# Delta-rule attention with two feed-forward blocks: inverse blocks through TensorE, doubling in the solve, an order table per task

## Chip, cores and metric

One core of one Trainium2 chip runs the whole program. The metric is the device time of one execution in microseconds (us). TensorE does matmuls, VectorE (DVE in the profile) and ScalarE (ACT) element-wise work, GpSimd (POOL) also element-wise work, and SyncE (SP) issues DMAs.

## What is computed

```python
# q, k, v: (4, 8, 768, 48); beta: (4, 8, 768)
k_n = k / (norm(k, axis=-1) + 1e-6)
for t in range(768):                              # per batch and head
    y[t] = q[t] @ state                           # state: 48 x 48
    state += beta[t] * outer(k_n[t], v[t] - k_n[t] @ state)
x = y, heads side by side                         # 3072 tokens x 384
h = x @ moe_w_in                                  # 384 x 2048
g = where(h >= 1, h, where(h <= -1, 0, (h + 1)**2 / 4))
x = g @ moe_w_out                                 # 2048 x 384
xn = x / sqrt(mean(x*x) + 1e-6) * rms_g
return (silu(xn @ w_gate) * (xn @ w_val)) @ w_out # 384 x 1536, back to 384
```

q, k, v and beta are float32, the weights 64-bit floats, which are decoded on the chip into a high and a low part, so that each product is three matmuls.

## The kernel before, in words

The sequence is cut into 12 chunks of 64 tokens. A unit u is one chunk c = u // 2 for half of the batch (p = u % 2); its tiles hold two batch elements on the two halves of the 128 partitions and eight heads beside each other. Within a chunk the recurrence is a triangular system: the Gram matrix of the keys, scaled by beta and the norms, is inverted, and everything else is matmuls.

The work is written as generator tasks. Each `yield S(engine, cost, needs, acquire, release)` is a stage, with an estimated cost and the buffers (tokens) that it takes and returns. `Flow` (lines 57 to 160) runs over all tasks when the program is built, simulates the engines with these costs and so fixes the order of instructions on each engine. A task's priority is the one given in `fl.add` plus an offset from the table `PLACE`, which is kept by chunk, feature block or group. Names in `CHAIN` go ahead of everything when they are ready. On TensorE lateness counts first; then `KEEP` and `STAY` favour staying with the kind of matmul that runs, small tiles (`TILED`) or full ones.

The tasks: `a_ss` loads k and sums its squares, `a_coef` (line 381) makes the coefficients, `ka_load` loads transposed keys, and `a_gram` (line 415) computes the Gram blocks (tile gk). For the groups g = 0 and 1 (chunks 0 and 1) `a_gram` scales them into al (L438), stores them to DRAM (L440) and keeps a masked copy off (L444). `inv16` then inverts the 16x16 diagonal blocks of a whole chunk: eight gathers from DRAM put one block on each partition (L469), 15 steps of two operations solve (L475, L481; on VectorE for chunk 0, on GpSimd for chunk 1), a copy (L483) and two DMAs through DRAM (L486, L489) bring the inverse back as c, and L499 multiplies it into dt. Later chunks go through `inverse`, `a_mz` and `a_mw`, with GpSimd as the solver (L526, L532). The attention itself is `b_load`, `b_q`, `b_vn`, `b_gs`, `b_tr`, `b_x`, `b_ds`; `b_xT` transposes the result into xh and xl. `b_tr` of chunks 0 and 1 multiplies with dt (L640) and off (L648).

The first feed-forward block is `m1(j, f)` over seven token blocks j (the first two are one chunk of 256 tokens each, then two chunks each) and 16 feature blocks f: hps, the activation on ScalarE and VectorE (L780 to L791), then acc three features behind; all big matmuls are L743 to L745. A weight piece comes through `w_dec`: a load (L279), three ScalarE operations (L286 to L288) and three more (L296, L302 or L300, L304). The 32 pieces of the first block stay in the 32 buffers of the pool wp, which before that also lends its buffers to early tiles (`early`). SyncE's queue is in order. The stages that load weights, keys or queries name `("inv16", 0, 1)` or `("inv16", 0, 19)` among their needs, that is the gathers or the end of chunk 0's solve. Until the first `m1`, gaps on TensorE are filled with dummy matmuls on the tile warm (L876). From `m2_l1` on the second feed-forward block runs in a fixed order without the planner.

## Time and profile before

| | us |
|---|---|
| median of three runs | 1097.67 (1097.43 to 1098.48) |
| profiled execution | 1095.42 |
| its span, first to last instruction | 1093.7 |
| TensorE matmul busy | 1071.0 (98%) |
| VectorE busy | 625.6 (57%) |
| ScalarE busy | 517.1 (47%) |
| GpSimd busy | 261.2 (24%) |

A stretch is read with the windows view, which gives each engine's busy time in it and the granted TensorE clock as a share of full speed. Dummy matmuls count as busy, and a busy matmul may overlap the next one, so the distance from start to start tells what one costs. The timeline view gives the order of instructions with start, duration and, in brackets, the idle time before and what ended it.

### The profile page before, as it was taken

What the parts mean: (1) busy time and instruction counts of PE and PEld (TensorE: products, weight loads), DVE (VectorE), ACT (ScalarE), POOL (GpSimd) and SP (SyncE); (2) the same over time, 40 slices, a digit from 0 to 9 for tenths busy, and PEclk for the clock granted to TensorE, in tenths of its full rate; (3) what the DMA queues carried; (4) which work ended last, traced back from release to release, by engine and by line L of the source; (5) the groups of instructions that cost most, each with busy time, mean ns of one, the idle gap of its engine ahead of it and who ended that gap; (6) DMA issues with size and microseconds to landing.
All of it is one profiled execution on the core that took longest, in us unless ns stands there. A gap on an engine that the chain in (4) does not pass through costs nothing.

```text
span 1093.7 us, 23824 instructions
## 1 busy us (share of the span) xinstructions
PE 1071.0 (98%) x9872; PEld 905.7 (83%) x9872; DVE 625.6 (57%) x1132; ACT 517.1 (47%) x981; POOL 261.2 (24%) x438
## 2 busy tenths in 40 slices
PE   8989799999999999999999999999999999999998
PEld 8878798988887888888888888888888888888886
DVE  6878988866677656855666533633333333333332
ACT  4676866756556557557656542522222122222221
POOL 3137849478286581100000000000000000000000
PEclk9998999999999999999999999999999999999999
DMA  7896575865755725353334930100010010010000
GB/s 220 268 283 191 130 174 170 192 179 165 191 163 135 206 88 128 115 165 107 109 114 174 330 111 10 40 30 29 0 39 20 1 49 10 22 36 1 30 1 29
DMA packets 156700, 121.84 MB, mean 111 GB/s; under 512 B 111408, under 2 KB 122288, under 8 KB 156592
## 3 DMA queue, kind: packets, MB, share of 16 engines
q1 hardware_dynamic: 134400, 117.60, 36.0%
q10 hardware_dynamic: 22192, 2.72, 1.8%
q8 instruction: 78, 1.28, 0.5%
q14 instruction: 30, 0.25, 0.1%
HBM read 86.21 MB, written 34.08 MB: 110 GB/s over the span
## 4 chain that ended last, share of the span: by engine, by line
PE 87%; DVE 4%; DMA 4%; ACT 2%; issue 1%; SPq 1%; POOL 0%; ACTq 0%; DVEq 0%; POOLq 0%
PE acc L743 11%; PE acc L744 10%; PE acc L745 10%; PE gv L744 9%; PE gv L743 9%; PE gv L745 9%; PE hps L743 6%; PE hps L744 6%; PE hps L745 6%; PE gs L619 3%; PE tr L683 2%; PE px L696 2%; PE ds L710 1%; DMA kvb<-in_kv 1%; PE mg L575 1%
## 5 line engine op out<-in xcount | busy, mean ns | idle before, releaser
L743 PE MATMUL acc<-g,w 128*128 128x512 f32 (+1 forms) x552 | 209.6, 380 | 0.0
L744 PE MATMUL acc<-g,w 128*128 128x512 f32 (+1 forms) x552 | 205.2, 372 | 0.3 <-DVE g L791 0.3
L745 PE MATMUL acc<-g,w 128*128 128x512 f32 (+1 forms) x552 | 204.7, 371 | 0.0
L745 PE MATMUL gv<-fix,w 128*128 128x512 f32 x432 | 168.1, 389 | 0.0
L743 PE MATMUL gv<-fix,w 128*128 128x512 f32 x432 | 168.0, 389 | 0.0
L744 PE MATMUL gv<-fix,w 128*128 128x512 f32 x432 | 168.0, 389 | 0.0
L760 ACT ACTIVATE g<-fix 128x512 fp32r<-128x512 f32 x72 | 45.4, 631 | 211.4 <-PE acc L745 203.9
L743 PE MATMUL hps<-xh,w 128*128 128x512 f32 (+1 forms) x336 | 126.1, 375 | 0.3 <-DVE s L783 0.3
L761 DVE TENSOR_TENSOR g<-fix,g 128x512 fp32r<-128x512 f32 x72 | 49.9, 693 | 131.8 <-ACT g L760 131.8
L744 PE MATMUL hps<-xl,w 128*128 128x512 f32 (+1 forms) x336 | 121.5, 362 | 0.0
L745 PE MATMUL hps<-xh,w 128*128 128x512 f32 (+1 forms) x336 | 121.4, 361 | 0.0
L743 PEld LDWEIGHTS acc<-g,w 128*128 128x128 f32 x552 | 103.8, 188 | 20.4
L745 PEld LDWEIGHTS acc<-g,w 128*128 128x128 f32 x552 | 103.9, 188 | 18.2
L744 PEld LDWEIGHTS acc<-g,w 128*128 128x128 f32 x552 | 103.9, 188 | 17.4 <-DVE g L791 0.7
L783 DVE TENSOR_TENSOR s<-s,hps 128x512 f32<-128x512 f32 (+1 forms) x112 | 67.8, 608 | 86.3 <-ACT s L781 85.4
L780 ACT ACTIVATE s<-hps 128x512 f32<-128x512 f32 (+1 forms) x112 | 59.8, 534 | 108.6 <-PE hps L745 96.2
L526 POOL TENSOR_TENSOR tmp<-nt,xi 128x31 f32<-128x31 f32 (+15 forms) x155 | 92.8, 599 | 46.7 <-DMA nt<-scr_a 35.0
L983 DVE TENSOR_TENSOR fix<-fix,gv 128x512 f32<-128x512 f32 x72 | 49.5, 687 | 87.4 <-ACT fix L982 87.4
L532 POOL TENSOR_TENSOR xi<-xi,tmp 128x31 f32<-128x31 f32 (+15 forms) x155 | 94.2, 608 | 12.1
L743 PEld LDWEIGHTS gv<-fix,w 128*128 128x128 f32 x432 | 81.1, 188 | 16.9
L745 PEld LDWEIGHTS gv<-fix,w 128*128 128x128 f32 x432 | 81.1, 188 | 16.8
L744 PEld LDWEIGHTS gv<-fix,w 128*128 128x128 f32 x432 | 81.1, 188 | 16.7
(162 smaller groups left out, 1648.5 us busy)
## 6 DMA issues: line engine op xcount, KB each, us to landing
wst<-in_w SPq DMA_DIRECT2D x68, 384.0 KB
w2d<-wst SPq DMA_DIRECT2D x36, 384.0 KB
w<-w2d SPq DMA_DIRECT2D x36, 384.0 KB
kvb<-in_kv SPq DMA_DIRECT2D x22, 384.0 KB
kt<-in_kqT SPq DMA_DIRECT2D x24, 256.0 KB
scr_a<-al SPq DMA_DIRECT2D x24, 256.0 KB
qs<-in_kqT SPq DMA_DIRECT2D x48, 128.0 KB
xn_d<-x SPq DMA_DIRECT2D x12, 384.0 KB
```

Source lines behind the costliest of these rows:

```text
L526: nc.gpsimd.tensor_tensor(out=tv, in0=nt[:, m:32, j:m].to_broadcast([w, n, m]), in1=x[:, j:m, 0:m].to_broadcast([w, n, m]), op=ALU.mult,)
L532: nc.gpsimd.tensor_tensor(out=x[:, m:32, 0:m], in0=x[:, m:32, 0:m], in1=tv, op=ALU.add)
L619: nc.tensor.matmul(out=ps[half(b), h, 0:n], lhsT=kt[u][half(1 - b), 4 * k + h, :], rhs=qs[p][half(1 - b), b, 4 * k + h, 0:n], start=True, ...
L683: nc.tensor.matmul(out=ps[half(b), h, 0:D], lhsT=w[half(b), h, :], rhs=r[half(b), h, :], start=True, stop=True)
L743: nc.tensor.matmul(out=out, lhsT=wh, rhs=xh, start=first, stop=False, skip_group_check=shared)
L744: nc.tensor.matmul(out=out, lhsT=wh, rhs=xl, start=False, stop=False, skip_group_check=shared)
L745: nc.tensor.matmul(out=out, lhsT=wl, rhs=xh, start=False, stop=last, skip_group_check=shared)
L760: nc.scalar.activation(out=hi, in_=src, func=ACTF.Copy)
L761: nc.vector.tensor_tensor(out=lo, in0=src, in1=hi.bitcast(F32), op=ALU.subtract)
L780: nc.scalar.activation(out=s, in_=ps, func=IDENTITY_SAT240, scale=240.0)
L783: nc.vector.tensor_tensor(out=s, in0=s, in1=ps, op=ALU.max)
L983: nc.vector.tensor_tensor(out=sg, in0=sg, in1=ps[0], op=ALU.mult)
```

## The change

For chunks 0 and 1 the scaled Gram block no longer goes through DRAM. `a_gram` writes e1, the block times a table mcoef that keeps only the diagonal 16x16 blocks (coefficients and signs included). `inv16` gathers with 64 matmuls of e1 against a selection matrix pick_t into PSUM (tile nps), which a copy brings to nt. The solve writes into x as before; for chunk 0 it now inverts 4x4 blocks in three steps and then doubles the size twice (4 to 8, 8 to 16), each with two products and two sums; chunk 1 keeps the 15 steps on GpSimd. A new task `inv_t` spreads x with a mask mlow (e2) and brings it back with 32 matmuls against pick_g (tile cps), from which dt is made. The constant tables come from the identity matrix with five VectorE operations. The first loads of k are issued at the very start, those of kt on ScalarE's queue. The needs that name `inv16` at other tasks' loads are gone. `PLACE` has an entry for every task, in the order in which tasks are added; `CHAIN` is longer, and `KEEP`, `STAY` and `AHEAD` are other numbers. In the diff the table and repeated edits are left out.

```diff
--- before.py
+++ after.py
-    TILED = ("a_gram", "a_mw", "b_gs", "b_tr", "b_x", "b_ds")
-    CHAIN = {"b_tr": 2, "b_x": 6, "inverse": 3, "inv16": 2, "a_mz": 2, "a_mw": 3, "b_gs": 1, "a_ss": 2, "b_ds": 1, "a_gram": 1}
-    DRAIN, SWITCH, KEEP, STAY, AHEAD = 0.15, 0.22, 25.96, 0, 0.17
+    TILED = ("a_gram", "a_mw", "b_gs", "b_tr", "b_x", "b_ds", "inv16", "inv_t")
+    CHAIN = {"a_gram": 6, "a_mw": 3, "a_mz": 9, "a_ss": 3, "b_ds": 3, "b_gs": 3, "b_load": 28, "b_q": 7, "b_tr": 9, "b_vn": 6, "b_x": 2, "b_xT": 30, "inv16": 13, "inv_t": 18, "inverse": 3, "w_in": 12, "x_load": 14}
+    DRAIN, SWITCH, KEEP, STAY, AHEAD = 0.15, 0.22, 229.72, 19.85, 0.27
     PLACE = {
...
     }
     def add(self, prio, fn, *args):
         gen, n = fn(*args), fn.__name__
+        i = self.seen[n] = self.seen.get(n, -1) + 1
         if n in self.PLACE:
-            prio += self.PLACE[n][args[0] // 2 if n in self.BY_UNIT else args[0]]
+            prio += self.PLACE[n][i]
         self.live.append([prio, (n, *args), gen, next(gen), 0])
 
...
     mdiag = cst([128, 4], "mdiag")
+    mlow = cst([128, 4], "mlow")
+    pick_t = cst([128, 16], "pick_t")
+    pick_g = cst([128, 16], "pick_g")
+    mcoef = [cst([128, 2 * H, 4], f"mcoef{c}") for c in range(2)]
...
     def consts():
+        for p in range(NP):
+            kv_b[p] = p2.tile([128, 2, DM], F32, name="kvb", tag="kvb")
+            nc.sync.dma_start(out=kv_b[p][:, 0], in_=kv[p, 0, :, 0])
         nc.sync.dma_start(out=beta_sb, in_=beta)
+        for p in range(NP):
+            kt[p] = p2.tile([128, H, C], F32, name="kt", tag="kt")
+            nc.scalar.dma_start(out=kt[p], in_=kqT[p, 0, :, 0])
...
     def consts2():
+        make_identity(nc, ident)
+        neg = early([128, C], "neg")
+        nc.vector.scalar_tensor_tensor(out=neg, in0=ident[:, 0:C], scalar=-1.0, in1=ident[:, C:], op0=ALU.mult, op1=ALU.subtract)
+        for t, v in (
+            (mdiag, neg.rearrange("p (x t) -> p x t", t=16)), (pick_t, neg.rearrange("p (x t) -> p t x", t=16)),
+            (pick_g, neg.rearrange("p (g x) -> p g x", x=4)), (mlow, neg.rearrange("p (g x) -> p x g", x=4)),
+        ):
+            nc.vector.reduce_sum(t, v, axis=mybir.AxisListType.X)
...
             needs = [("a_gram", EARLY - 1)] if f + SK * i > 14 else []
-        if n == 1:
-            needs = needs + ([("inv16", 0, 1 if f + SK * i < 9 else 19)] if f + SK * i >= 4 else [])
...
-            yield S("SP", (1, 0.55), [("inv16", 0, 1 if u < 4 else 19)], mem)
+            yield S("SP", (1, 0.55), (), mem)
...
+        if g < 2:
+            nc.vector.tensor_tensor(
+                out=mcoef[g], in0=bc(nn.rearrange("p u h -> p (u h)"), 4), in1=mdiag.unsqueeze(1).to_broadcast([128, 2 * H, 4]), op=ALU.mult
+            )
+            return
...
-            yield S("SP", (1, 0.73), (), ("kt",))
-            ka_t[u] = kt[u] = p2.tile([128, H, C], F32, name="kt", tag="kt")
-            nc.sync.dma_start(out=kt[u], in_=kqT[p, c, :, 0])
+            yield S("SP", (0, 0.73), (), ("kt",))
+            ka_t[u] = kt[u]
...
-        if g > 1:
-            yield S("ACT", 1.7, [("a_coef", g)], ("wp" if ew else "al",), ("at",), alt=[("DVE", 0.68)])
-        else:
-            yield S("DVE", 0.68, [("a_coef", g)], ("wp",))
+        if g < 2:
+            yield S("DVE", 0.7, [("a_coef", g)], ("wp",))
+            off["e", u] = e1 = early([128, 16 * 4 * H], "e1")
+            nc.vector.tensor_tensor(
+                out=e1.rearrange("p (s m) -> p m s", s=16), in0=ps.rearrange("p h (x s) -> p (h x) s", s=16),
+                in1=bc(mcoef[g][:, H * i:H * i + H].rearrange("p h x -> p (h x)"), 16), op=ALU.mult,
+            )
+            yield S("DVE", 0.68, [("inv16", 0, 0)] + ([("a_gram", u - 1)] if u else []), ("wp",) if g else ("wt",), (bank, "wp") if u == 3 else (bank,))
+            off[u] = early([128, H, C], "off") if g else p2.tile([128, H, C], F32, name="off", tag="wt")
+            nc.vector.tensor_tensor(out=off[u], in0=ps, in1=off["m"].unsqueeze(1).to_broadcast([128, H, C]), op=ALU.mult)
+            return
+        yield S("ACT", 1.7, [("a_coef", g)], ("wp" if ew else "al",), ("at",), alt=[("DVE", 0.68)])
...
     def inv16(c):
         us = (2 * c, 2 * c + 1)
-        name, eng = ("POOL", nc.gpsimd) if c else ("DVE", nc.vector)
         if c:
-            yield S("POOL", 1.0, [("inv16", 0)], ("tx", "tx", "z", "z"))
-        else:
-            yield S("POOL", 2.0, (), ("tx", "tx", "z", "z", "wp"))
+            yield S("POOL", 1.0, [("inv16", 0)], ("tx", "tx", "wp"))
+        else:
+            yield S("POOL", 1.4, (), ("tx", "tx", "wp", "wp"))
             off["m"] = moff = early([128, C], "moff")
             nc.gpsimd.memset(moff, -1.0)
-            nc.gpsimd.memset(mdiag, -1.0)
             for b in range(2):
-                for t, base, pat, cm in ((moff, -16, [[-16, 4], [0, 16]], 1), (mdiag, 0, [[-16, 4]], 1), (mdiag, 15, [[16, 4]], -1)):
-                    nc.gpsimd.affine_select(
-                        out=t[half(b)], in_=t[half(b)], compare_op=ALU.is_ge, fill=0.0, base=base, pattern=pat, channel_multiplier=cm
-                    )
-        x = p2.tile([128, 16, 16], F32, name="x0", tag="tx")
+                nc.gpsimd.affine_select(
+                    out=moff[half(b)], in_=moff[half(b)], compare_op=ALU.is_ge, fill=0.0, base=-16, pattern=[[-16, 4], [0, 16]], channel_multiplier=1
+                )
+        nt, x = (p2.tile([128, 272], F32, name=nm, tag=tag) for nm, tag in (("nt0", "g21"), ("x0", "tx")))
+        off["x", c] = x
+        xv, nv = (t[:, 0:256].rearrange("p (t s) -> p t s", s=16) for t in (x, nt))
         nc.gpsimd.memset(x, 0.0)
-        nc.gpsimd.affine_select(out=x, in_=x, compare_op=ALU.not_equal, fill=1.0, base=0, pattern=[[1, 16], [-1, 16]], channel_multiplier=0)
-        yield S("SP", (5, 2.4), [("a_gram", u, 2) for u in us])
-        nt = p2.tile([128, 16, 16], F32, name="nt0", tag="g21")
-        for k in range(8):
-            o, r = 16 * k, 16 * (k % 4)
-            q = nc.scalar if k in (1, 3, 5) else nc.sync
-            q.dma_start(out=nt[o:o + 16], in_=scr_a[c][o:o + 16, :, :, r:r + 16].rearrange("t u h s -> (u h) t s"))
-        tmp = p2.tile([128, 64], F32, name="tmp0", tag="tx")
-        for j in range(15):
-            n, m = 15 - j, j + 1
-            yield S(name, 0.5 + n * m * 0.006 if c else 0.37 + n * m * 2 / 960)
-            tv = tmp[:, 0:n * m].rearrange("p (a b) -> p a b", a=n)
-            eng.tensor_tensor(
+        nc.gpsimd.affine_select(out=xv, in_=xv, compare_op=ALU.not_equal, fill=1.0, base=0, pattern=[[1, 16], [-1, 16]], channel_multiplier=0)
+        for k, u in enumerate(us):
+            yield S("PE", 1.35, [("a_gram", u, 1)], () if k else ("at",), ("wp",))
+            if k == 0:
+                ps = ap_.tile([128, 16, 16], F32, name="nps", tag="at")
+            e1 = off.pop(("e", u)).rearrange("p (s m) -> p s m", s=16)
+            for r in range(16):
+                for b in range(2):
+                    o = 64 * b + 32 * k
+                    nc.tensor.matmul(out=ps[o:o + 32, r, :], lhsT=e1[half(b), r, :], rhs=pick_t[half(b)], start=True, stop=True)
+        yield S("ACT" if c else "DVE", 0.43, (), (), ("at",))
+        if c:
+            nc.scalar.activation(out=nv, in_=ps.rearrange("p s t -> p t s"), func=ACTF.Copy)
+        else:
+            nc.vector.tensor_copy(nv, ps.rearrange("p s t -> p t s"))
+        tmp = early([128, 512], "tmp0")
+        if c:
+            for j in range(15):
+                n, m = 15 - j, j + 1
+                yield S("POOL", 0.45 + n * m * 0.0058)
+                tv = tmp[:, 0:n * m].rearrange("p (a b) -> p a b", a=n)
+                nc.gpsimd.tensor_tensor(
+                    out=tv,
+                    in0=nv[:, m:16, j:m].to_broadcast([128, n, m]),
+                    in1=xv[:, j:m, 0:m].to_broadcast([128, n, m]),
+                    op=ALU.mult,
+                )
+                nc.gpsimd.tensor_tensor(out=xv[:, m:16, 0:m], in0=xv[:, m:16, 0:m], in1=tv, op=ALU.add)
+            return
+
+        def blocks(t, w):
+            return t.rearrange("p (k r) -> p k r", r=17 * w)[:, :, 0:16 * w].rearrange("p k (t s) -> p k t s", s=16)
+
+        n4, x4 = blocks(nt, 4), blocks(x, 4)
+        for j in range(3):
+            n, m = 3 - j, j + 1
+            yield S("DVE", 0.4)
+            tv = tmp[:, 0:4 * n * m].rearrange("p (k a b) -> p k a b", k=4, a=n)
+            nc.vector.tensor_tensor(
                 out=tv,
-                in0=nt[:, m:16, j:m].to_broadcast([128, n, m]),
-                in1=x[:, j:m, 0:m].to_broadcast([128, n, m]),
+                in0=n4[:, :, m:4, j:m].to_broadcast([128, 4, n, m]),
+                in1=x4[:, :, j:m, 0:m].to_broadcast([128, 4, n, m]),
                 op=ALU.mult,
             )
-            eng.tensor_tensor(out=x[:, m:16, 0:m], in0=x[:, m:16, 0:m], in1=tv, op=ALU.add)
-        yield S("DVE", 0.6)
-        nc.vector.tensor_copy(nt, x.rearrange("p t s -> p s t"))
-        yield S("SP", (1, 1.5))
-        scr = dram.tile([16, 8, 2, H, 16], F32, name=f"scr_{c}", tag=f"scr_{c}")
-        nc.sync.dma_start(out=scr.rearrange("s x u h t -> (x u h) s t"), in_=nt)
-        yield S("SP", (1, 0.5))
-        inv["c"] = cc = p2.tile([128, 2 * H, 16], F32, name="c0", tag="z")
-        nc.sync.dma_start(out=cc, in_=scr.rearrange("s x u h t -> x s (u h t)"))
-        yield S("DVE", 1.08, ["consts2"], ("x2",))
-        m = p2.tile([128, 2 * H, 4], F32, name="m0", tag="g21")
-        nn = coef[c][1].rearrange("p u h -> p (u h)")
-        nc.vector.tensor_tensor(out=m, in0=bc(nn, 4), in1=mdiag.unsqueeze(1).to_broadcast([128, 2 * H, 4]), op=ALU.mult)
+            nc.vector.tensor_tensor(out=x4[:, :, m:4, 0:m], in0=x4[:, :, m:4, 0:m], in1=tv, op=ALU.add)
+        half_t = p2.tile([128, 64], F32, name="half", tag="tx")
+        for w in (4, 8):
+            q = 8 // w
+            nw, xw = blocks(nt, 2 * w), blocks(x, 2 * w)
+            tv = tmp[:, 0:q * w**3].rearrange("p (k i j l) -> p k i j l", k=q, i=w, j=w)
+            hv = half_t[:, 0:q * w * w].rearrange("p (k i j) -> p k i j", k=q, i=w)
+            for lhs, rhs, out in ((nw[:, :, w:2 * w, 0:w], xw[:, :, 0:w, 0:w], hv), (xw[:, :, w:2 * w, w:2 * w], hv, xw[:, :, w:2 * w, 0:w])):
+                yield S("DVE", 0.37 + 2 * q * w**3 / 960)
+                for k in range(q):
+                    nc.vector.tensor_tensor(
+                        out=tv[:, k],
+                        in0=lhs[:, k].unsqueeze(2).to_broadcast([128, w, w, w]),
+                        in1=rhs[:, k].rearrange("p l j -> p j l").unsqueeze(1).to_broadcast([128, w, w, w]),
+                        op=ALU.mult,
+                    )
+                nc.vector.reduce_sum(out, tv, axis=mybir.AxisListType.X)
+
+    def inv_t(c, i):
+        yield S("POOL" if c else "DVE", 1.1 if c else 0.72, [("inv16", c)], ("wp",))
+        eng = nc.gpsimd if c else nc.vector
+        e2 = early([128, 512], "e2").rearrange("p (t x s) -> p t x s", t=8, x=4)
+        xv = off["x", c][:, 128 * i:128 * i + 128].rearrange("p (t s) -> p t s", s=16)
+        eng.tensor_tensor(
+            out=e2, in0=xv.unsqueeze(2).to_broadcast([128, 8, 4, 16]),
+            in1=bc(mlow, 16).unsqueeze(1).to_broadcast([128, 8, 4, 16]), op=ALU.mult,
+        )
+        yield S("PE", 1.15, [("inv_t", c, 0)] if i else (), () if i else ("at",), ("wp",) if i else ("wp",))
+        if i == 0:
+            off["c", c] = ap_.tile([128, 16, 16], F32, name="cps", tag="at")
+        ps = off["c", c]
+        for t in range(8):
+            for b in range(2):
+                nc.tensor.matmul(
+                    out=ps[half(b), 8 * i + t, :], lhsT=e2[half(b), t].rearrange("p x s -> p (x s)"), rhs=pick_g[half(b)], start=True, stop=True
+                )
+        if i == 0:
+            return
         inv[c] = x2p.tile([128, 2 * H, 4, 16], F32, name="dt", tag="x2")
+        cc = ps.rearrange("p t g -> p g t")
         for p in range(2):
             hs = slice(H * p, H * p + H)
-            if p:
-                yield S("DVE", 0.69, (), (), ("tx", "tx", "z", "z"))
+            yield S("DVE", 0.69, (), () if p else ("x2",), ("at", "tx", "tx", "wp") if p else ())
             nc.vector.tensor_tensor(
                 out=inv[c][:, hs],
                 in0=cc[:, hs].unsqueeze(2).to_broadcast([128, H, 4, 16]),
-                in1=m[:, hs].unsqueeze(3).to_broadcast([128, H, 4, 16]),
+                in1=mcoef[c][:, hs].unsqueeze(3).to_broadcast([128, H, 4, 16]),
                 op=ALU.mult,
             )
 
...
-            yield S("PE", 0.98, [("inv16", c, 20 + p), ("b_vn", u)] + gs, ("at",))
+            yield S("PE", 0.98, [("inv_t", c, 1, 2 + p), ("b_vn", u)] + gs, ("at",))
...
+            for i in range(2 * (g < 2)):
+                fl.add(p0 + 7 + i, inv_t, g, i)
```

## Rows read from the trace of the kernel before

**Rows 1.** Windows, busy us: PE, PEld, DVE, ACT, POOL (x instructions); clock, DMA share, GB/s

```profile
0.00:5.00 5.00, 2.77 (x13) 2.78 (x14) 0.54 (x9) 2.58 (x5) 3.81 (x21) 1.00 0.46 141
5.00:20.00 15.00, 14.86 (x167) 14.49 (x167) 10.26 (x22) 8.22 (x18) 4.37 (x5) 1.00 0.70 222
20.00:66.00 46.00, 42.47 (x921) 39.34 (x920) 39.95 (x103) 26.48 (x59) 12.73 (x34) 1.00 0.93 277
66.00:140.00 74.00, 63.27 (x955) 58.14 (x955) 63.37 (x126) 55.01 (x123) 44.34 (x67) 0.93 0.67 181
140.00:200.00 60.00, 58.52 (x1074) 55.43 (x1070) 52.05 (x113) 38.84 (x95) 43.05 (x72) 1.00 0.69 188
200.00:600.00 400.00, 399.29 (x4595) 330.25 (x4594) 266.04 (x478) 248.74 (x460) 152.86 (x240) 1.00 0.52 147
```

**Rows 2.** Windows of the filler matmuls alone (tile warm), TensorE, to 66 us

```profile
0.00:66.00 66.00, 32.75 (x248) 30.54 (x248) 1.00 0.84 254
```

**Rows 3.** Timeline, chunk 0: start us, us, engine, line, operation, operands, count [idle before]

```profile
8.69 0.69 DVE L438 TENSOR_TENSOR al<-gk,nn 128x512 f32<-128x512 f32 x1 [0.90 <-PE gk L427]
...
20.12 0.17 DVE L475 TENSOR_TENSOR tmp<-nt,x 128x15 f32<-128x15 f32 x1
...
27.94 0.48 DVE L483 COPY nt<-x 128x256 f32<-128x256 f32 x1
...
28.45 0.39 SPq L486 DMA_DIRECT2D scr<-nt  x1
...
31.96 0.69 SPq L489 DMA_DIRECT2D c<-scr  x1
...
36.47 1.29 DVE L499 TENSOR_TENSOR dt<-c,m 128x512 f32<-128x512 f32 x2
...
37.78 2.07 PE L640 MATMUL tr<-kvb,dt 64*64 64x48 f32 x64
...
64.80 0.39 PE L743 MATMUL hps<-xh,w 128*128 128x256 f32 x1
```

**Rows 4.** Timeline and chain of work, chunk 1: GpSimd, a load, two TensorE waits

```profile
50.23 0.24 POOL L475 TENSOR_TENSOR tmp<-nt,x 128x15 f32<-128x15 f32 x1 [21.38 <-DVE w L302]
...
73.46 7.09 DMA c<-scr
...
83.35 1.95 PE L640 MATMUL tr<-kvb,dt 64*64 64x48 f32 x32 [3.52 <-DVE qs L629]
...
134.62 1.76 PE L619 MATMUL gs<-qs,kt 64*64 64x112 f32 x16 [2.44 <-DVE qs L629]
```

**Rows 5.** Groups by line, L304 (busy us, mean ns), 9-66 and 87-137 us; timeline, last one

```profile
L304 DVE TENSOR_TENSOR w<-dy,w 128x384 fp32r<-128x384 f32 x13 | 7.6, 606 | 0.2
...
L304 DVE TENSOR_TENSOR w<-dy,w 128x384 fp32r<-128x384 f32 x14 | 11.0, 783 | 0.3
...
139.22 0.56 DVE L304 TENSOR_TENSOR w<-dy,w 128x384 fp32r<-128x384 f32 x1
```

**Rows 6.** Groups by form, VectorE solve step, 20 to 28.5 us: busy, mean ns

```profile
L475 DVE TENSOR_TENSOR tmp<-nt,x 128x64 f32<-128x64 f32 x1 | 0.8, 818 | 0.0
...
L475 DVE TENSOR_TENSOR tmp<-nt,x 128x63 f32<-128x63 f32 x2 | 0.4, 224 | 0.1
```

**Rows 7.** Timeline, TensorE, one change to small matmuls and back

```profile
149.99 0.28 PE L744 MATMUL hps<-xl,w 128*128 128x256 f32 x1
150.11 0.28 PE L745 MATMUL hps<-xh,w 128*128 128x256 f32 x1
150.32 1.20 PE L565 MATMUL mg<-tx,g 32*32 32x32 f32 x64
151.45 0.38 PE L743 MATMUL acc<-g,w 128*128 128x256 f32 x1
151.67 0.28 PE L744 MATMUL acc<-g,w 128*128 128x256 f32 x1
151.79 0.28 PE L745 MATMUL acc<-g,w 128*128 128x256 f32 x1
```

More of the change, by code (lines that the diff above doesn't have):

```diff
@@ L89 @@
+        "x_load": (-0.2,),
     }
@@ L361, in a_ss @@
         if c == 0:
[L362 to L363 removed]
+            yield S("SP", (0, 0.55), (), ("kvb",))
             k_in = kv_b[u][:, 0]
         else:
[L366 removed]
+            yield S("SP", (1, 0.55), (), mem)
             k_in = kk = early([128, DM], "kk") if u < EARLY else p2.tile([128, DM], F32, name="kk", tag="kk")
[L368 removed]
+            nc.sync.dma_start(out=k_in, in_=kv[p, c, :, 0])
         if c == 0:
@@ L440, in a_gram @@
         nc.sync.dma_start(out=scr_a[g][:, i], in_=al)
-        if g < 2:
-            yield S("DVE", 0.68, [("inv16", 0, 1)] + ([("a_gram", u - 1)] if u else []), ("wp",) if g else ("wt",), (bank, "wp") if u == 3 else (bank,))
-            off[u] = early([128, H, C], "off") if g else p2.tile([128, H, C], F32, name="off", tag="wt")
-            nc.vector.tensor_tensor(out=off[u], in0=ps, in1=off["m"].unsqueeze(1).to_broadcast([128, H, C]), op=ALU.mult)
     def inv16(c):
         us = (2 * c, 2 * c + 1)
-        name, eng = ("POOL", nc.gpsimd) if c else ("DVE", nc.vector)
```

96 lines of the change are left out of this document (66 added, 30 removed), and 15 rows, old and new, of the table PLACE.

## Prediction

> **What bounds the kernel now.** I read the windows view first, a table of busy time by stretch, because one average over the span hides stages with different limits [rows 1]. TensorE is busy 399.29 of 400 us between 200 and 600 us, so there only less TensorE work can shorten anything. Before 140 us the picture differs. TensorE idles 5.00 - 2.77 = 2.2 us in the first stretch, 0.1 us to 20 us, 46.00 - 42.47 = 3.5 us to 66 us and 74.00 - 63.27 = 10.7 us to 140 us: 16.6 us. A part of what counts as busy is filler: 248 dummy matmuls take 32.75 us, all before 66 us [rows 2]. The granted clock of 0.93 between 66 and 140 us [rows 1] means 2 x 0.07 x 74 = 10 us at the lower level of 1.2 GHz, where half of the time, 5 us, is lost; the two falls follow the waits of 3.52 and 2.44 us at 83.35 and 134.62 us [rows 4]. Together TensorE loses 16.6 + 32.75 + 5 = 54 us by 140 us. After that it loses 1.5 us to 200 us and 0.7 us to 600 us. So the end is set by when TensorE becomes saturated, and by how much of its work is then done.
>
> What delays saturation has two parts. The first is the chain of chunk 0, in the timeline [rows 3]: the scaled Gram block is on VectorE at 8.69 us, but its 16x16 blocks come back through DRAM in the wanted layout only at 20.12 us, the 15-step solve lasts until 27.94 us, and two more trips through DRAM end with dt at 36.47 us. The first product with dt is at 37.78 us, the first useful big matmul (hps) at 64.80 us. The second is the decoding of the w1 weights. Chunk 0 needs all 32 pieces, and the last is ready at 139.22 + 0.56 = 139.8 us [rows 5]; the next chunk can't go ahead of it. VectorE bears that: 0.54 + 10.26 + 39.95 + 63.37 = 114.1 us busy by 140 us, 25.9 us idle [rows 1].
>
> **The change, part by part.** *Chunk 0's layout and solve.* Removed on the way are the store of al, the eight gathers, 30 short VectorE operations and a copy, the store and load of c. In their place: e1 on VectorE (a product over 128x512 like al, 0.69 us each, [rows 3]), 64 small matmuls, a copy, the solve by doubling, then two e2 products, 32 matmuls, and dt as before. The matmuls: 64 of 32x32 took 1.20 us in a row [rows 7], so the 64 first ones cost 1.2 us and the 32 others, of larger tiles, 0.6 to 1.2 us. The doubling has 6 short operations (0.22 us each, by the 128x63 row of [rows 6]) = 1.3 us, at width 4 four short products and two sums, at most 6 x 0.3 = 1.8 us, at width 8 two products over 512 elements and two sums over as many, 4 x 0.65 = 2.6 us by dt's 1.29 us for two [rows 3]: 5.7 us where 7.8 us were. The trace shows no sum with this stride, so I bound it by a half more, 8.5 us. From e1 at about 8.5: two e1 1.4, matmuls and hops 1.5, copy 0.6, solve 5.7, e2 1.4, matmuls 1.2, hops 1.0, so dt begins near 21.5 us instead of 36.47: 15 us earlier, 12 with the slow sums. The earlier first loads (k and kt are issued ahead of everything, kt on ScalarE's queue instead of SyncE's) are worth up to 1 us of that and are included in the 8.5.
>
> *Waits on SyncE's queue.* Loads of weights and of later chunks no longer wait for chunk 0's gathers. In 5 to 20 us VectorE is busy only 10.26 of 15 us [rows 1], because it has five weight pieces and nothing more to decode; that gap can now be filled. 18 DMAs leave SyncE's queue and 6 ScalarE's; two kt loads move to ScalarE, ahead of its first activation, at some 0.4 us each, hidden since the squares wait for k anyway. No wait is added on SyncE.
>
> *Chunk 1* loses the same trips: its solve on GpSimd begins at 50.23 us though its Gram block is much earlier, and c alone flies 7.09 us from 73.46 us [rows 4]. TensorE then stands 3.52 us. This goes; what is next late are the weights. The new tiles nps and cps take one of three PSUM banks (at) until copied out or multiplied into dt; behind them the attention matmuls queue. In a stretch where TensorE has spare time this costs 0 to 2 us. I take 0.
>
> *What of the 15 us reaches the end.* Not all: once hps starts early, chunk 0 is paced by the weights, and that is VectorE's work. The change leaves VectorE about as much of it (minus 7.8, the copies and m; plus 5.7, e2, copy, constants: 0 within 2 us). So the last decoded piece moves by the idle time that goes, out of 25.9 us. By name: about 3.5 of the 4.7 us between 5 and 20 us; some 5 of the 6.0 us between 20 and 66 us; some 3.5 of 10.6 us between 66 and 140 us (the wait for c, and what hung on TensorE's stall). Sum 12 us, the piece at 128 instead of 140 us. Bounds: 4 us (only the gaps that the c loads made) and 18 us. Everything after that point is TensorE's, so the end moves by the same 12 us.
>
> *TensorE's added work.* Chunk 0's half lies in stretches that are filler today: nothing. Chunk 1's 96 matmuls cost 2 us and two changes of tile shape, 0.6 us, but partly in spare time: 1 us, between 0 and 3.
>
> *The order.* The per-chunk offsets become per-task ones, and the rule for leaving a tile shape is stiffer both ways (STAY 0 to 19.85, KEEP 25.96 to 229.72). A change of shape and back costs about 0.3 us: 0.21 instead of 0.12 us into the small ones, 0.22 instead of 0.12 us after the first big one, and about 0.1 us at their end [rows 7]. There are 77 such groups after 65 us, 49 of them after 200 us: 25 us in all. A stiffer rule should merge some; I take ten, 3 us (bounds 1 us lost, 9 us gained).
>
> Sum: -12 + 1 - 3 = -14 us. The profiled execution took 1095.42 us (span 1093.7), so 1081.4 us; it lies 2.25 us below the median of the three runs, 1097.67 us, which makes **1083.7 us** by the median.
>
> *A rule against it.* One short VectorE product took 818 ns where its neighbours of nearly the same size took 224 ns [rows 6]. At length, the last decoding step takes 606 ns a piece in the stretch before 66 us and 783 ns in the one where GpSimd solves [rows 5]. The Trainium skill has a rule for it (SBUF — State Buffer, "Who interferes with whom"): a VectorE instruction with two SBUF inputs contends with a GpSimd instruction that reads SBUF. By that rule the trace agrees, and it is the first rival below.
>
> **The rivals.** *A. VectorE gets slower as GpSimd's solves slide over the decoding.* The last decoding step is 783 instead of 606 ns when they meet, a quarter longer [rows 5]. Today half of the pieces escape. If ten more pieces and the solve of chunk 0 meet GpSimd's, each piece's three steps cost some 0.5 us more, 5 us, and the queues behind another 3 us: of 12 us 4 stay, and the order gives nothing: 1097.67 - 3 = 1095 us. Against it: GpSimd's total work is unchanged, and chunk 1's solve falls on earlier time. Chance 0.13.
>
> *B. The new order opens holes in the saturated stretch.* If small groups are held back until full ones are late, the chain of a later chunk comes late, and TensorE stands before its first hps. Between 200 and 600 us it now loses 0.7 us over 49 groups [rows 1], so there is everything to lose. From 14 / 49 = 0.29 us a group the gain is gone; at 0.5 us a group it is 24.5 - 14, some 1108 us. Against it: lateness is weighed ahead of every preference for TensorE. Chance 0.10.
>
> *C. The whole early shift arrives.* The hps start moves by 15 us and more, VectorE's idle time shrinks to its first 5 us and the order merges 25 groups: -20 + 1 - 8 = -27, 1071 us. For it: 54 us are lost before 140 us [rows 1, 2], far more than 27. Chance 0.15.
>
> *D. The chain isn't shortened*, because PSUM banks or VectorE's queue hold the new steps: then only the freed loads act, and it is A's time; it is counted there.
>
> **How the numbers follow.** The forecast, 1083.7 us, has 0.62, its own range 1074 to 1093 us. A measurement can tell about 0.2%, 2.2 us, from no change. Slower by more is B, 0.10; within it is half of A, 0.06; faster is the rest, 0.84. The range of 8 in 10 takes in most of C and A and leaves out B: 1067 to 1096 us.
>
> **What would show it.** Right: dt of chunk 0 near 21 to 24 us, hps near 45 to 50 us, the last w1 piece near 128 us, filler near 20 us, TensorE's loss between 200 and 600 us still under 2 us, fewer than 70 groups after 65 us. The step for the weights is wrong if the last piece comes near 138 us although hps starts early; the forecast as a whole fails if idle time shows up after 200 us.

## The result and the profile after

The change makes the kernel 1.4% slower: 1112.25 us median (1110.51 to 1116.66, four runs) beside 1097.84 us (1097.43 to 1098.48) for the kernel before on the same chip. The ratio is 1.0137, 95% interval 1.0107 to 1.0167. The forecast was 1083.7 us. The profiled execution took 1116.66 us, 21.2 us more than the profiled one of before; the medians lie 14.4 us apart, so the account of these two traces holds more than the typical loss.

The windows of the changed kernel answer to [rows 1], in the same stretches and columns (us busy on PE, PEld, DVE, ACT, POOL, then the clock, the DMA share and GB/s). The last line counts the filler alone, as in [rows 2].

```profile
0.00:5.00 5.00, 3.58 (x17) 3.58 (x17) 1.48 (x14) 2.21 (x4) 3.84 (x17) 1.00 0.60 184
5.00:20.00 15.00, 13.92 (x323) 12.78 (x324) 13.26 (x31) 4.70 (x10) 4.22 (x5) 0.89 1.04 295
20.00:66.00 46.00, 39.68 (x925) 36.89 (x919) 34.87 (x78) 24.35 (x58) 12.45 (x35) 0.88 0.81 286
66.00:140.00 74.00, 65.72 (x1126) 61.25 (x1122) 65.56 (x129) 57.18 (x127) 43.50 (x67) 0.89 0.62 166
140.00:200.00 60.00, 54.61 (x868) 51.99 (x866) 44.56 (x95) 33.55 (x82) 42.32 (x72) 0.86 0.59 161
200.00:600.00 400.00, 395.00 (x4650) 328.76 (x4649) 261.34 (x476) 250.21 (x468) 153.27 (x241) 0.99 0.54 146
...
0.00:66.00 66.00, 21.13 (x132) 18.93 (x132) 0.89 0.85 280
```

TensorE's loss is read as in the prediction: idle time, filler, and 1 minus the clock times the stretch (at 1.2 GHz half of the time is lost). Up to 140 us: 1.4 + 1.1 + 6.3 + 8.3 = 17.1 us idle, 21.1 us filler, 1.7 + 5.5 + 8.1 = 15.3 us by the clock, 53.5 us in all, where before lost 54. Some 12 us less filler stand beside 10 us more lost by the clock. From 140 to 200 us it loses 5.4 + 8.4 = 13.8 us (before 1.5), and from 200 to 600 us 5.0 us idle and some 4 us by the clock (before 0.7). So nothing was gained early, and some 20 us were lost in a stretch that was full before.

The timeline of chunk 0 (start us, duration us, engine, line, operation, operands, count) answers to [rows 3]; the last two lines are VectorE's first and last finished piece of w1, to be read beside [rows 5].

```profile
9.27 1.03 DVE L506 TENSOR_TENSOR e<-gk,mcoef 128x512 f32<-128x512 f32 x1
...
10.35 1.19 PE L550 MATMUL nps<-pick_t,e 64*32 64x16 f32 x64 [0.62 <-DVE e L506]
...
14.52 0.17 DVE L579 TENSOR_TENSOR tmp<-nt,x 128x12 f32<-128x12 f32 x1
...
20.89 1.44 DVE L608 TENSOR_TENSOR e<-x,mlow 128x512 f32<-128x512 f32 x2
...
26.41 1.29 DVE L628 TENSOR_TENSOR dt<-cps,mcoef 128x512 f32<-128x512 f32 x2
...
45.78 0.85 PE L791 MATMUL tr<-z,y 32*32 32x48 f32 x15 [3.71 <-issue]
...
56.45 0.55 PE L857 MATMUL xps<-ident,xs 128*128 128x128 f32 x3
...
72.16 0.49 PE L857 MATMUL xps<-ident,xs 128*128 128x128 f32 x3
74.98 0.36 PE L872 MATMUL hps<-xh,w 128*128 128x256 f32 x1
...
36.61 0.56 DVE L376 TENSOR_TENSOR w<-dy,w 128x384 fp32r<-128x384 f32 x1
...
148.79 0.56 DVE L376 TENSOR_TENSOR w<-dy,w 128x384 fp32r<-128x384 f32 x1
```

The chain to dt is 10 us shorter (26.41 beside 36.47 us). But dt to hps takes 48.6 us instead of 28.3, the first piece of w1 is ready at 37.2 us (before 12.6, the line below) and the last at 149.4 us (before 139.8): without the old needs the new order lets the loads of attention go ahead of the weights, and weaves chunk 1's steps into chunk 0's chain.

```profile
12.01 0.56 DVE L304 TENSOR_TENSOR w<-dy,w 128x384 fp32r<-128x384 f32 x1
```

The waits of TensorE from 140 to 260 us (engine, line, what for: us in all, times, longest) show the late loss; before had none of these three in this stretch.

```profile
PE px L825 <- ACT qs L815: 3.8, 1, 3.8
PE gs L748 <- DMA qs<-in_kqT: 2.6, 1, 2.6
PE mg L694 <- DMA g<-scr_a: 1.6, 1, 1.6
```

The waits of SyncE's queue (one line, 130 to 240 us), the timeline of the engines around 164 us, and three windows behind it, in that order:

```profile
SPq L486 <- PE gk L502: 12.0, 2, 8.1
...
155.52 1.15 PE L502 MATMUL gk<-ka 64*64 64x64 f32 x32
162.41 0.97 PE L502 MATMUL gk<-ka 64*64 64x64 f32 x26
...
163.60 0.38 SPq L486 DMA_DIRECT2D ka<-in_kqT  x1
164.04 1.70 SPq L351 DMA_DIRECT2D wst<-in_w  x2
165.78 0.91 SPq L439 DMA_DIRECT2D kk<-in_kv  x2
166.79 0.53 SPq L675 DMA_DIRECT2D tx<-scr_x  x1
...
169.19 0.55 ACT L358 ACTIVATE dy<-wst 128x384 f32<-128x384 f32 x1 [5.94 <-DMA wst<-in_w]
170.60 1.96 ACT L815 ACTIVATE qs<-tr 64x384 f32<-64x384 f32 x4
171.61 1.95 PE L825 MATMUL px<-qs 128*64 128x48 f32 x32 [3.78 <-ACT qs L815]
175.17 1.07 PE L694 MATMUL mg<-tx,g 32*32 32x32 f32 x32 [1.61 <-DMA g<-scr_a]
...
170.00:175.00 5.00, 1.95 (x32) 1.79 (x32) 2.27 (x5) 4.91 (x12) 1.36 (x3) 0.61 0.79 215
175.00:180.00 5.00, 4.83 (x76) 4.51 (x77) 4.96 (x7) 2.87 (x8) 4.69 (x7) 0.50 0.62 199
180.00:190.00 10.00, 10.00 (x181) 9.29 (x181) 7.74 (x19) 3.45 (x9) 8.98 (x14) 0.59 0.47 147
```

Read from below: px waits for ScalarE's eviction of tr; ScalarE stands before that eviction in a decode whose weights haven't landed; those weights were issued at 164.04 us because SyncE held the ka load ahead of them until the gram at 162.41 us was done. That load itself waited 8.1 us. One load in the wrong place of one queue stopped three engines. Then the clock is 0.61, 0.50 and 0.59 in the three windows, 3.9 + 5.0 + 8.2 = 17.1 us at 1.2 GHz, while TensorE alternates short stretches of small and large tiles.

### The profile page after: what moved, and what is told of

Same layout as the page of the kernel before. It is cut to its first block, busy times and chain, and to the rows that moved or that the text cites. A ratio compares the mean times of both kernels' runs of the same rounds, so it can differ in the third digit from the quotient of the medians.

```text
span 1114.9 us, 24348 instructions
## 1 busy us (share of the span) xinstructions
PE 1083.6 (97%) x10146; PEld 918.3 (82%) x10146; DVE 623.5 (56%) x1121; ACT 521.2 (47%) x992; POOL 259.6 (23%) x435
## 4 chain that ended last, share of the span: by engine, by line
PE 86%; POOL 4%; DMA 3%; DVE 3%; SPq 2%; issue 1%; ACT 0%; POOLq 0%; DVEq 0%
PE acc L872 10%; PE acc L873 10%; PE acc L874 10%; PE gv L872 9%; PE gv L873 9%; PE gv L874 9%; PE hps L872 6%; PE hps L873 5%; PE hps L874 5%; PE gs L748 3%; PE px L825 2%; POOL xi L661 2%; POOL tmp L655 2%; PE tr L812 2%; SPq L646 2%; PE ds L839 1%
## 5 line engine op out<-in xcount | busy, mean ns | idle before, releaser
L872 PEld LDWEIGHTS acc<-g,w 128*128 128x128 f32 x552 | 105.3, 191 | 19.4
L874 PEld LDWEIGHTS acc<-g,w 128*128 128x128 f32 x552 | 105.6, 191 | 18.3
L873 PEld LDWEIGHTS acc<-g,w 128*128 128x128 f32 x552 | 105.5, 191 | 17.8 <-DVE g L920 1.0
```

The costliest lines, as they stand in the source:

```text
L872: nc.tensor.matmul(out=out, lhsT=wh, rhs=xh, start=first, stop=False, skip_group_check=shared)
L873: nc.tensor.matmul(out=out, lhsT=wh, rhs=xl, start=False, stop=False, skip_group_check=shared)
L874: nc.tensor.matmul(out=out, lhsT=wl, rhs=xh, start=False, stop=last, skip_group_check=shared)
```

## Experiments

Names: "before" is the kernel before, "the change" the changed kernel. Each ratio is to before, measured beside it, with its interval. From e10 on (e20 apart) the kernels take every engine's steps from a written list, that of before or of the change, so that one step can be moved and all others keep their order. "Chunk 0 done" is the start of the next token block's first hps. Single traces scatter: in the change, e9, e10 and e11, whose edits all lie behind it, the first hps comes at 75.0, 73.4, 75.6 and 72.1 us, so a shift of up to 3.5 us of it in one trace says nothing.

**1. The path with the old order table (e1).** The planner plans anew, with the constants, chains and offsets of before and the old holds on the weights tied to the new steps.

```diff
-    DRAIN, SWITCH, KEEP, STAY, AHEAD = 0.15, 0.22, 229.72, 19.85, 0.27
+    DRAIN, SWITCH, KEEP, STAY, AHEAD = 0.15, 0.22, 25.96, 0, 0.17
-            prio += self.PLACE[n][i]
+            prio += self.PLACE[n][args[0] // 2 if n in self.BY_UNIT else args[0]]
```

> The new inverse path and the earlier first loads as in the change, but with the order of the kernel before (its offsets by chunk, CHAIN, KEEP, STAY, AHEAD) and its holds on the loads, tied to the new steps that bring the blocks. Theory O (the new order lost what the path gained): dt near 24 us, the first weight piece decoded near 13 us, hps before 58 us, the last piece before 136 us, and 1080 to 1092 us. Rival P (the path itself costs more than it saves, by PSUM banks, small matmuls and crowded loads): 1098 us or more, last piece after 140 us.

Measured: 1127.08 us, 1.0269 (1.0252 to 1.0287). Slower even than the change: dt at 25.6 us, first piece at 12.7, hps at 69.8, last piece at 142.7, but TensorE is busy 53.72 of 60 us from 140 us and 387.15 of 400 us from 200 us. Rival P's two marks are met, and still they don't show that the path costs this: e12 below has the same path in before's own order and is some 27 us faster. The old table opens holes of its own when the planner runs it on the new steps. So this run does not separate path and order. (The old path under the new table is not among the runs.)

**2. The rule for tile shapes alone (e20).** The same constants line in before, the other way round.

> The kernel before with the constants of the new batching rule alone (KEEP 229.72, STAY 19.85, AHEAD 0.27 instead of 25.96, 0 and 0.17); path, order table and chains as before, so the planner places TensorE's stages anew by the old table. Theory B (fewer changes of tile shape save about 3 us, as forecast): end 2 to 4 us earlier, 1094 to 1096, with fewer than 70 groups of small tiles behind 65 us (77 in the kernel before). Rival H (held groups make other engines wait): fewer groups, but as much or more idle time on TensorE behind 65 us (12.9 us before), end the same or later.

Measured: 1161.94 us, 1.0567 (1.0546 to 1.0589). 66 groups of small tiles after 65 us instead of 77, and TensorE busy 363.95 of 400 us from 200 us; the largest of its waits, in the timeline:

```profile
335.52 1.87 PE L683 MATMUL tr<-kvb,wt 64*64 64x48 f32 x27 [16.05 <-POOL wt L554]
```

Rival H holds: fewer groups, and far more idle time. The planner made the whole order anew, so how much of it comes from groups held back is not shown, and what the rule does with a table fitted to it is not shown either.

**3. Doubling, order of pieces, filler (e3, e6, e8).** Three single edits of the change: the solve in 15 steps as before; the w1 pieces in the order in which they are needed, in the same slots; more filler per gap.

```diff
-            for _ in range(max(0, int((gap - 0.2) / 0.23))):
+            for _ in range(max(0, int((gap + 0.3) / 0.115))):
```

> The change with chunk 0's solve in 15 steps again instead of doubling, the order unchanged. The doubling took 14.5 to 21.0 us in the change's trace, 15 steps took 7.8 us before, so dt comes 1 to 2 us later. Theory O: the end within 2 us of the change, 1110 to 1114 us. Rival P with the doubling as its cost: at least 5 us faster than the change, below 1107 us.

> The change, with the same loads and decoding steps at the same places, but the pieces of w1 go through them in the order in which chunk 0 needs them instead of the table's (1, 0, 5, 8, 3, ...). Theory O with the scrambled pieces as its main part: TensorE's work of chunk 0 is spread out better, and the end comes 4 us or more earlier, 1100 to 1108 us. Rival: only the last piece counts, it stays at 149 us, and the time is within 2 us of the change.

> The change with about twice as many filler matmuls in the same gaps before the first hps, the order of all else unchanged. Rival C (the lower clock in 44.8 to 55.1 and 65.3 to 72.1 us makes the way to hps late): less time at the lower clock, hps 4 us or more earlier and 1104 to 1109 us. Theory O: hps at most 3 us earlier, and the end within 3 us of the change, since the weights pace chunk 0.

Measured: 1110.29 us, 1.0117 (1.0091 to 1.0142); 1111.75 us, 1.0128 (1.0113 to 1.0143); 1144.12 us, 1.0427 (1.0406 to 1.0448). The first two are the change within its spread: neither the doubling (with 15 steps dt is at 28.6 instead of 26.4 us) nor the scrambled pieces carry the loss. The filler came out at 74.8 us instead of 23.1 (550 records instead of 138, four times as many and not twice). The clock stays at 2.4 GHz to 140 us, and hps comes at 110.6 us: both theories missed. In a chain of short steps the filler stands in front of the next step.

**4. The ka load (e10), and the next late load (e11).** The change with one, then two SyncE steps moved:

```diff
 SyncE's steps, plan of the change
-ka_load 20
 w_dec 2 5 1; w_dec 2 1 1; a_ss 21; a_ss 22; a_mz 7; a_mz 6
+ka_load 20
...
+b_q 8                  (e11 only)
 inverse 4, stage 1
-b_q 8
```

> The changed kernel with one DMA issue moved in SyncE's queue: the ka load of unit 20, which stood at 163.6 us for 8.1 us waiting for the gram of unit 16, goes behind the two weight loads, two kk loads and four tx and g loads that stood behind it. All else in the same order. Theory Q (that wait is what delays the weight loads, the decoding on ScalarE, the eviction of tr and so px and mg): the waits of 3.78 and 1.61 us and the 17.1 us at half clock after them go, 5.4 + 8.6 = 14 us, about 1098 us, and the second hidden chunk block is done near 210 instead of 224 us. Rival R (these loads would be late anyway because the work before them is 11 us late): within 4 us of 1112.

> As the run before, and the qs load of unit 8 goes ahead of the four nt loads of inverse 4, whose issue took SyncE 8.11 us at 224.1. Theory Q: the wait of 2.56 us at 236.4 and the 6.8 us at half clock after it go as well, 6 us more than the run with one move alone, about 1092 us. Rival R: the place of the wait moves to the next late load and less than 2 us are gained over the run with one move.

Measured: 1104.82 us, 1.0049 (1.0035 to 1.0064), and 1105.67 us, 1.0062 (1.0037 to 1.0087). TensorE in e10, the same products as above:

```profile
161.27 0.97 PE L859 MATMUL gk<-ka 64*64 64x64 f32 x26
...
166.61 1.14 PE L1182 MATMUL px<-qs 128*64 128x48 f32 x32
167.68 0.69 PE L1051 MATMUL mg<-tx,g 32*32 32x32 f32 x32
```

Neither waits, and px and mg take 1.14 and 0.69 instead of 1.95 and 1.07 us, at the full clock. The second hidden block is done at 214.1 instead of 224.0 us; 7.4 of the 14 us forecast arrive by the medians (9.7 by the ratios, 1.0137 and 1.0049). Theory Q holds for the ka load in its mechanism, with about half its size; for the qs load rival R does (gs then waits 3.4 us for VectorE instead).

Why the load stood there can be read in the code. A ka tile holds both units of a chunk, and a_gram's stage gives it back with `("ka",) if u % 2 else ()`, at the odd unit's gram. The old table puts the even gram first each time. The new one puts unit 17 ahead of unit 16 (155.52 and 162.41 us above), so the planner counts the tile as free one gram too early: its model has no wait where the chip waits 8.1 us.

**5. The clock (e9) and the filler (e14).** e9: matmuls of the identity in TensorE's queue ahead of the three waiting products. e14: e10 without the filler behind the first dt.

```diff
+        for _ in range({4: 30}.get(u, 0)):
+            nc.tensor.matmul(out=ps.rearrange("p h c -> p (h c)")[:, 0:128], lhsT=ident, rhs=ident, start=True, stop=True)
```

> The changed kernel with full-size matmuls of the identity on itself in TensorE's queue ahead of three matmuls that wait (30 ahead of px of unit 4, which waited 3.78 us at 171.6; 13 ahead of the first mg of unit 6, 1.61 us at 175.2; 21 ahead of the second half of gs of unit 8, 2.56 us at 236.4); they write the bank that the waiting matmul then overwrites. Order and waits are the same. Theory C (the waits are paid twice, once as idle time and once as the 17.1 and 6.8 us at 1.2 GHz that follow them): the clock stays at 2.4 GHz there, half of 23.9 us or about 12 us come back, about 1100 us. Rival N (the half clock comes from the small tiles that run behind the waits, not from the idle time): half-clock time unchanged, within 3 us of 1112. The idle time itself (8 us) stays in both.

> The changed kernel with the ka load moved as in e10_ka_later and without the 36 filler matmuls that stand behind the first dt (27 us on); 23 before it stay. Theory F (fillers stand in the way of chunk 0's chain): hps 4 to 8 us earlier than the 75.6 us of e10_ka_later, end 2 to 6 us earlier than its 1104.8. Rival G (the fillers hold the clock): more time at 1.2 GHz than the 42 us of e10_ka_later, the chain no earlier, end the same or later.

Measured: 1117.78 us, 1.0172 (1.0152 to 1.0192), and 1101.96 us, 1.0035 (1.002 to 1.0051). e9's fill came too late, since its first group itself waited for the bank that the eviction frees, and each of these matmuls is two records:

```profile
169.08 8.59 PE L826 MATMUL px<-ident 128*128 128x128 f32 x60 [3.81 <-ACT qs L819]
177.60 1.14 PE L831 MATMUL px<-qs 128*64 128x48 f32 x32
178.67 3.17 PE L692 MATMUL mg<-ident 128*128 128x128 f32 x26
...
196.22 0.97 PE L502 MATMUL gk<-ka 64*64 64x64 f32 x26
```

So it says nothing of the total, but it prices the clock. The time at 1.2 GHz behind the wait falls from 17.1 to 3.4 us, and the same products, from px to the next gram, take 196.22 - 177.60 - 3.17 = 15.5 us; in the change it is 194.66 - 171.61 = 23.1 us, of which 1.6 us are the wait for mg. The low clock cost 6 us there, more than the wait of 3.8 us ahead of it. Neither theory holds as put. The wait of 3.81 us was still there and still brought the low clock, for 3.4 us, so C's remedy was not tested; but with full-size matmuls behind the wait the half-clock time did not stay as N had it. The fill also covered the second wait, that for mg, so whether that wait or the small tiles kept the clock low in the change is not separated. e14: hps at 73.0 us lies inside the scatter of this point (72.1 to 75.6 us), the end is 2.9 us earlier than e10's by the medians and 1.5 by the ratios, whose intervals overlap, and the time at 1.2 GHz grew from 42 to 48 us. F is not shown; G's "end the same" is not excluded.

**6. The path in the order of before (e12, e13, e17).** The list of before with the DRAM steps replaced. In e12 the new steps take the places of the old; in e13 chunk 0's chain moves up to the new dt; in e17 the first four hidden groups move up as well.

```diff
 TensorE's steps, before -> e13 (e17: the last two lines swap places)
-warm x55; gs 0 0; gs 0 1; warm x2; gs 1 0; warm x7; gk 2; gk 3; gs 1 1; warm x31; tr 0; tr 1; ...
+nps 0; warm x6; gs 0 0; gs 0 1; warm x12; cps 0; warm x3; tr 0; tr 1; warm x7; gk 2; gk 3; ...
+... xps 1; gk 6; nps 1; gk 4; gk 5; gk 7
+hps of f = 0 to 3
```

> The new path alone in the old order: every engine takes the steps of before in the very order of before, with the DRAM hops of the first two chunks replaced by the TensorE steps and the solve by doubling at the place of the old one (35 fewer filler matmuls, as the waits they filled are shorter). Theory O (the path is worth what was forecast, and the new order table is what loses): dt near 26, hps near 53 to 57, last piece of w1 near 130, end at 1080 to 1092 us. Rival P (the path itself costs, or an earlier chunk 0 only moves waits): 1095 us or more, with hps early and idle time of TensorE between 65 and 300 us above the 12.2 us that the old kernel has there.

> The new path in the old order once more, with the first chunk's chain moved up to where the path now lets it start: cps right behind the first gs, tr of units 0 and 1 right behind dt, ahead of the grams of units 2 and 3, the chain's evictions on ScalarE and VectorE ahead of the decodes that stood before them, nearly no filler, chunk 1's nps behind the last xps of chunk 0, and the grams of units 10 and 11 behind the first two hps groups. Theory O (the path is worth what was forecast once the chain really starts at dt): hps near 50 to 56, chunk 0 done near 128, no wait for dt of chunk 1 near 73 to 83, end at 1083 to 1092 us. Rival P (chunk 0 is bound by the decoding of w1, so an early hps only waits): hps near 52, chunk 0 done at 136 or later, end within 5 us of before.

> The path in the old order with its chain early (e13_path_tight), and now the first four hidden groups of chunk 0 as well some 11 us earlier in every queue: the first hps right behind the first gram after the last xps, ahead of chunk 1's nps and four grams. Theory T (TensorE was idle or slow for want of work it could have had): first hps near 52 to 55, chunk 0 done 4 or more us before 137, end at 1088 to 1094. Rival W (the end of chunk 0 is held elsewhere, by the decoding of w1 and the GpSimd inverse that ScalarE waits for at 131): first hps near 52 to 55, chunk 0 done at 136 to 140 all the same, end within 3 us of before.

Measured: 1100.17 us, 1.0022 (1.0008 to 1.0036); 1099.19 us, 1.0005 (0.9991 to 1.0019); 1100.28 us, 1.0031 (1.0012 to 1.0051). e12 still started tr at 38.3 us behind filler and a gram that waited 3.4 us, and hps at 72.0 us, far from the 53 to 57 of theory O. In e13 the chain is early:

```profile
24.03 0.94 PE L1362 MATMUL warm<-ident 128*128 128x128 f32 x6
25.69 2.07 PE L1126 MATMUL tr<-kvb,dt 64*64 64x48 f32 x64 [0.73 <-DVE dt L985]
...
49.38 1.52 PE L1196 MATMUL ds<-z,kvb 64*48 64x48 f32 x32 [4.08 <-issue]
50.82 0.90 PE L1214 MATMUL xps<-ident,xs 128*128 128x128 f32 x3
53.82 3.42 PE L907 MATMUL nps<-pick_t,e 64*32 64x16 f32 x128 [0.19 <-DVE qs L1203]
...
64.42 0.58 PE L1229 MATMUL hps<-xh,w 128*128 128x256 f32 x1
...
139.07 0.56 DVE L733 TENSOR_TENSOR w<-dy,w 128x384 fp32r<-128x384 f32 x1
```

tr at 25.69 instead of 37.78 us, the last xps at 50.8 instead of 58.1, and then hps at 64.42 (64.80), the last piece at 139.6 (139.8), chunk 0 done at 137.3 (138.1), the second block at 201.6 (202.3): the trace of before again, within 1 us. Two numbers say where the time went. TensorE lost 13.4 us idle, 14.5 us filler and 10.4 us by the clock up to 66 us, 38.3 us, as before (5.9 + 32.75 = 38.7); and the new matmuls take 5.5 + 5.0 us, in two groups:

```profile
L907 PE MATMUL nps<-pick_t,e 64*32 64x16 f32 x256 | 5.5, 196 | 1.0 <-DVE e L863 0.8 <-DVE qs L1203 0.2
L975 PE MATMUL cps<-pick_g,e 64*64 64x16 f32 x128 | 5.0, 223 | 1.2 <-POOL e L965 1.2
```

```profile
53.70 0.38 PE L1229 MATMUL hps<-xh,w 128*128 128x256 f32 x1 [0.25 <-ACT xh L1223]
...
146.66 0.56 DVE L733 TENSOR_TENSOR w<-dy,w 128x384 fp32r<-128x384 f32 x1
```

e17 (these two lines) has hps at 53.7 us, and chunk 0 is done at 145.8, later than before: what was pushed back (nps, cps and dt of chunk 1, now at 91.7, the grams whose results SyncE and GpSimd wait for) is late in its turn, and the last piece comes at 147.2 us. T falls; W's sign holds, its 136 to 140 us don't. Over the three runs the first hps lies at 72.0, 64.4 and 53.7 us and the end within 0.4% of before's: when hps starts does not set the end.

**7. What holds the end of chunk 0 in before's order (e15, e16, e18, e19).** e15 and e16 move the cast of 16 late w1 pieces from VectorE to ScalarE, in before and in e13; e18 moves a ScalarE copy that waits for GpSimd's inverse behind two evictions in before, e19 does so in e17.

```diff
-w_dec 1 f i, stage 3 on VectorE      (16 pieces, e15 in before, e16 in e13)
+w_dec 1 f i, stage 3 on ScalarE
-inverse 2, stage 33 (nt from xi); m1 0 13, stage 1; m1 0 14, stage 1; w_dec 1 15 1, stage 1
+m1 0 13, stage 1; m1 0 14, stage 1; w_dec 1 15 1, stage 1; inverse 2, stage 33   (e18, e19)
```

> The kernel before, all in its own order, with one step of the decoding of w1 moved from VectorE to ScalarE for the last 16 pieces that had it on VectorE (the cast to fp32r, 16 of 0.556 us between 66 and 140 us; ScalarE takes 0.512 us for it and had 19 us without work in that stretch). Theory V (what sets the last piece of w1, and with it the end of chunk 0, is the amount of VectorE's work up to there, and not the time of chunk 0's inverse): last piece near 133 to 136 instead of 139.8, chunk 0 done 3 to 6 us earlier, end at 1092 to 1096 beside 1098. Rival S (loads or the needs of chunk 0's own chain set it): last piece unchanged within 1.5 us, end the same.

> The new path in the old order with its chain early (e13_path_tight), and the same 16 casts on ScalarE. Theory V: the last piece moves from 139.6 to 133 to 136, and the end to 1091 to 1096. Rival S: both unchanged within 1.5 us; then the early chain waits for something else than VectorE.

> The kernel before with one ScalarE step moved: the copy of GpSimd's inverse of units 4 to 7 (nt from xi, 2.06 us, for which ScalarE waited 2.08 us at 129 to 131) goes behind two hps evictions and one decode that stood behind it. Theory W (that wait holds the last groups of chunk 0): the wait of gs for VectorE at 132.2 to 134.6 and the 3.4 us at half clock behind it go, end 2 to 4 us earlier, near 1094 to 1096. Rival X (the next link of the same inverse, its DRAM hop and the mg of chunk 2, comes 2 to 3 us later and takes it back): end within 1 us.

> e17_hps_first and the move of e18_nt_later together. If T and W both hold in part: end at 1086 to 1092, faster than both kernels. If neither: within 3 us of before.

Measured: e15 1097.76 us, 1.0013 (0.9999 to 1.0026); e16 1099.40 us, 1.0017 (1.0001 to 1.0033); e18 1099.28 us, 1.0011 (0.9995 to 1.0027); e19 1105.05 us, 1.0069 (1.0047 to 1.0092). None gains. In e15 VectorE has 8 us more idle time between 66 and 140 us, and spends it on waiting for the engine that took the work:

```profile
DVE w L662 <- ACT w L658: 9.9, 14, 2.9
```

The last piece comes at 140.6 us, in e16 at 142.9. Theory V as I put it falls: VectorE's amount of work alone doesn't set it. So does W in e18: the last piece is at 142.7 us and the end does not move. With each of these suspects taken away, the end stays or moves back. That would fit several chains that end within a few us of each other, but no run shows it: what holds the last piece near 140 us stays open.

## Why the prediction was wrong, point by point

- **The outcome** is rival B's, slower by idle time behind 140 us, and near its 1108 us, but not by its mechanism, so the nearness is luck. B counted half a us for each of 49 groups held back; the groups of small tiles are 73 instead of 77, so little was held back, and the largest hole is a load at the head of SyncE's queue, then the low clock behind it. The forecast's sentence "No wait is added on SyncE" looked only at the waits that the diff removes. A new order adds waits without a line that says so, and this one is worth 7.4 us by the medians (e10).
- **"So the last decoded piece moves by the idle time that goes"** is the step that failed first, and with it the term of -12 us. In before's order, with the first product with dt 12 us earlier and the chain's end 7 us (e13), the last piece stays at 139.6 us and the ratio is 1.0005 (0.9991 to 1.0019): the term is nothing. In the change the piece comes at 149.4 us, not 128. VectorE's 25.9 idle us [rows 1] were no store to draw on: e13 still has 23.8, in other places. The prediction's own mark against this step, a last piece near 138 us although hps starts early, is met and passed in e17 (hps at 53.7, piece at 147.2 us). "So the end moves by the same 12 us" fails too: in e17 the piece is 7.4 us late and the end 3.4 us (1.0031). What does hold the piece is open, as said under 7, and no run shows that another order could not turn the early chain into an earlier end.
- **The path's length.** dt at 26.4 instead of 21.5 us. The two e1 took 1.03 us each where I took al's 0.69 [rows 3] (its write is strided; that this is the reason is not tested), the solve 6.5 us against 5.7 (inside its bound), cps 1.9 us against 1.2 with 1.5 us of filler and queue ahead of it. About half of the 4.9 us is lost ahead of the solve: its first product is at 14.52 us where the sum gives 12.0, since e1 starts 0.8 us later and VectorE does other work between e1 and the copy.
- **TensorE's added work**, +1 us, was mis-sized at its root. In [rows 7] the 64 records of mg are 32 matmuls of two records each, so 64 such matmuls are 2.4 us and not 1.2. In the change nps and cps take 5.1 + 4.1 = 9.2 us, in e13 10.5 us, half of it in chunk 1, where I priced 1.
- **The order**, -3 us, is the second step that failed: the rule alone, with the old table, costs 63 us (e20), table and rule together some 14 us (1.0137 against e13's 1.0005). The sign was wrong, and my bound of 1 us lost was no bound: I priced the changes of shape and not the waits that a different order makes. The ka load is the one such wait whose move brought time, and e10 still lies 4.8 us above e13 by the ratios; that rest is not traced.
- **Rival A**, VectorE slowed beside GpSimd, did not happen. The last decoding step takes 554 ns a piece in the first eight and 711 ns between 87 and 150 us, beside 606 and 783 ns (87 to 137 us) before [rows 5]. The rule of the Trainium skill that I weighed (SBUF — State Buffer, "Who interferes with whom") may stand for the difference between the two stretches; it did not grow.
- **What I said would show it**: filler near 20 us (21.1) and nothing else came. "The forecast as a whole fails if idle time shows up after 200 us" was the right mark, and the idle time starts at 168 us already.

## What to carry to other kernels

Time saved on a chain counts only if the next thing that the bound engine waits for comes earlier too: name it, and who must deliver it, before booking the saving. Here the prediction named the last weight piece, and it did not move. An order table is part of the kernel: judge it as a change of its own, by listing for each queue what now stands behind an instruction that waits. Where a planner counts buffers, check that its release is the last reader in the new order, as for the ka tile here.
